# Mamba-2 scan and hash-routed experts on one core: a new program with a 64-step factored scan and experts by seven quarter products

## The chip, the core and the metric

One NeuronCore of a Trainium2 chip runs the kernel; the other cores are idle. The time is the device time of one execution in microseconds (us). TensorE (PE) multiplies matrices, VectorE (DVE), ScalarE (ACT) and GpSimd (POOL) work element by element, and SyncE (SP) issues DMAs, as ACT and POOL also can. PEld is TensorE's loading of the stationary operand, which is recorded apart from the multiplication.

## What is computed

Two stages. The first is a scan over 4 sequences, 8 heads, 768 steps, head dimension 32 and state dimension 16; the second sends every token (a step with its 8 x 32 values) to one of 8 experts, chosen by a hash of the token's number. Cut to the core:

```python
# scan, per sequence and head; la = log(a)
cum = cumsum(la)                       # inside a chunk
M = (C @ B.T) * exp(cum_i - cum_j)     # zero where i < j
y = M @ x + (C @ state) * exp(cum_i)
state = exp(sum(la)) * state + sum_j B_j x_j exp(cum_end - cum_j)
# experts: N = 3072 tokens, 256 -> 1024 -> 256
e = token_ids * 2654435761 % 8
out[mask] = maximum(x[mask] @ w1[e], 0) @ w2[e]
```

Everything is float32. The result doesn't depend on where the chunks of the scan end.

## The kernel before

**Scan (lines 263 to 385).** The 3072 tokens are 24 chunks of 128 steps; chunk `gc` belongs to sequence `gc // 6`. `prepare` (L275 to L297) turns a sequence's B and C so that head and state lie on the partitions, 16 rows a head. `chunk` takes four heads at a time. For the decays it builds 128x128 triangles scaled by log a (`rl`, L316 on ACT and L318 on DVE), sums them on TensorE (`seg`, L320 and L322, 512 columns), takes the exponential (`dl`, L324), multiplies C.B (`gram`, L329) by it (`m`, L331), and multiplies the result, as a stationary 128x128 operand, with 32 columns of x (`y_ps`, L335). The state's share comes from L342 to L351, the state itself from `tp` at L358 and `s_new` at L364. Each chunk's y goes to DRAM by token (`y_tokens`, L352). In L358 four products fill the four groups of 32 columns of the array, one for each pair of heads.

**Routing.** `routing` (L190 to L249) finds every token's slot: experts stand one after the other, each from a multiple of 128 on, 31 slot tiles in all. 24 indirect DMAs (L252) write token numbers to their slots in DRAM, one load (L258) brings the table back, and `idx_in` (L259) is taken from it on DVE.

**Experts (L388 to L467).** A tile of 128 slots at a time: `gather` (L400) fetches rows of y by an indirect DMA on POOL, `turn_x` (L408) transposes them, `up` (L424) multiplies with the tile as stationary operand and w1 as moving, four products of 512 columns, then relu (L415, L417); `down` transposes h (L436), multiplies with w2 (L444), eight products of 256 columns, and scatters 128 rows (L448). All weights lie in SBUF; they are loaded on ACT's queue during the scan (`load_w`), two loads of 1 MB in every second chunk.

A scheduler orders each engine's instructions after the dependencies and the order in which the code issues them; each engine runs its own list in order. x, B, C and y go through SP's queue.

Of the kernel before, what the change touches and what calls it, by code (L numbers as in the profile page):

```python
# [9 lines left out]
F32 = mybir.dt.float32  # L10
# [8 lines left out]

@with_exitstack  # L20
def kernel(
# [11 lines left out]
    nc = tc.nc  # L33

# [33 lines left out]
    a_t = apre.tile([BH, S], F32)  # L68
    nc.sync.dma_start(out=a_t, in_=a.rearrange("b h s -> (b h) s"))

    bcs, xs = {}, {}

    def load_bc(b):
        t = aload.tile([P, 2, H, R * NS], F32, name="bc", bufs=1)
        for i, src in ((0, B), (1, C)):
            nc.sync.dma_start(out=t[:, i], in_=src[b].rearrange("h (p r) n -> p h (r n)", r=R))
        bcs[b] = t

    def load_x(gc):
        b, c = divmod(gc, R)  # L80
        t = aload.tile([P, H, D], F32, name="x_t", bufs=6)
        nc.sync.dma_start(out=t, in_=x[b, :, c * P:(c + 1) * P, :].rearrange("h p d -> p h d"))
        xs[gc] = t

    load_bc(0)
    XA = 4
    for gc in range(XA):
        load_x(gc)
# [3 lines left out]
    nc.sync.dma_start(out=tok, in_=tok_h.bitcast(I32).rearrange("(c p two) -> c p two", c=NCH, two=2))  # L92

    w1_sb = wpool.tile([P, E * WS], F32)
    w2_sb = wpool.tile([P, E * WS], F32)

    def load_w(e):
        s = slice(e * WS, (e + 1) * WS)
        nc.scalar.dma_start(out=w1_sb[:, s].rearrange("p (k f) -> p k f", k=DP),
                            in_=moe_w1[e].rearrange("(k p) f -> p k f", p=P))  # L100
        nc.scalar.dma_start(out=w2_sb[:, s].rearrange("p (k d) -> p k d", k=FP),
                            in_=moe_w2[e].rearrange("(k p) d -> p k d", p=P))

# [1 line left out]
    ident = const.tile([P, P], F32)  # L105
    make_identity(nc, ident)
    ident16 = const.tile([P, P], BF16)
    nc.vector.tensor_copy(out=ident16, in_=ident)
    ones = const.tile([P, P], F32)
    nc.vector.memset(ones, 1.0)  # L110
    upto = const.tile([P, P], F32)      # [k, i] = k <= i
    nc.gpsimd.affine_select(out=upto, in_=ones, pattern=[[1, P]], compare_op=OP.is_ge,
                            fill=0.0, base=0, channel_multiplier=-1)
    after = const.tile([P, P], F32)     # [k, j] = k > j
    nc.vector.tensor_scalar(out=after, in0=upto, scalar1=-1.0, scalar2=1.0, op0=OP.mult, op1=OP.add)
    low = const.tile([P, P], BF16)      # [j, i] = -1000 where i < j: exp of it is 0
    nc.vector.tensor_scalar(out=low, in0=upto, scalar1=1000.0, scalar2=-1000.0, op0=OP.mult, op1=OP.add)  # L117

    gmask = const.tile([P, G, 2 * D], F32)   # [(h n), g, :] = h // 2 == g
    nc.gpsimd.memset(gmask, 1.0)  # L120
    nc.gpsimd.affine_select(out=gmask, in_=gmask, pattern=[[-32, G], [0, 2 * D]], compare_op=OP.is_ge,
                            fill=0.0, base=0, channel_multiplier=1)
    nc.gpsimd.affine_select(out=gmask, in_=gmask, pattern=[[32, G], [0, 2 * D]], compare_op=OP.is_ge,
                            fill=0.0, base=31, channel_multiplier=-1)
    hm = const.tile([P, G, 2], F32)          # [(h n), g, e] = h == 2 g + e
    nc.gpsimd.memset(hm, 1.0)
    nc.gpsimd.affine_select(out=hm, in_=hm, pattern=[[-32, G], [-NS, 2]], compare_op=OP.is_ge,
                            fill=0.0, base=0, channel_multiplier=1)
    nc.gpsimd.affine_select(out=hm, in_=hm, pattern=[[32, G], [NS, 2]], compare_op=OP.is_ge,
                            fill=0.0, base=NS - 1, channel_multiplier=-1)  # L130
# [172 lines left out]
    def chunk(gc, s_old):  # L303
# [50 lines left out]
        if c == R - 1:  # L354
            return None
# [144 lines left out]
```

## Time and profile before

| | us |
|---|---|
| time, median of 3 runs | 505.13 (505.11 to 524.7) |
| span of the profiled execution | 506.3 |
| TensorE busy in it | 431.5 |
| VectorE, ScalarE, GpSimd busy | 160.9, 117.0, 93.0 |
| weights, 16 loads of 1 MB | 9.4 each, from issue to landing |

The span runs from the first to the last instruction. Busy times of engines overlap each other. A row of a timeline begins with its start and its length in us and merges neighbours of a kind (x8); the bracket is how long the engine stood idle before it and what ended that. A matrix product of float32 is recorded as two MATMULs with a LDWEIGHTS each.

### The profile page before, as it was taken

Reading aid. Unit: us, or ns where it says so; the run is one execution under the profiler, and the core shown is the slowest. Engines: PE = TensorE matmul, PEld = TensorE weight load, DVE = VectorE, ACT = ScalarE, POOL = GpSimd, SP = SyncE. Lnnn points to the kernel's source line nnn. Section 1 sums busy time; section 2 is a strip of 40 time slices with the busy share of each in tenths; the row PEclk is TensorE's granted clock in tenths of the full one; section 3 lists DMA queues with packets and bytes.
Section 4 is the critical chain, followed back from the end, with each engine's and each line's share of the span. In section 5 each row is a group of like instructions: output and inputs, shape, how many; then the busy total and the mean of one; then the engine's idle time right before and its main releaser. Section 6 shows DMA issues by size and latency. Waiting matters only on the chain.

```text
span 506.3 us, 6022 instructions
## 1 busy us (share of the span) xinstructions
PE 431.5 (85%) x2103; PEld 287.1 (57%) x2103; DVE 160.9 (32%) x399; ACT 117.0 (23%) x254; POOL 93.0 (18%) x106
## 2 busy tenths in 40 slices
PE   0689994008999999993999999999999999999992
PEld 0356652005656666662567676767667676767671
DVE  2355851003575675551112212121212122121210
ACT  2151441002344343420121212121121212121220
POOL 1100544500000000004331313132222222110110
PEclk9997998555999999996899999999999999999997
DMA  8966799625932112001110101010101111000000
GB/s 284 217 172 209 125 107 135 88 5 131 286 115 54 41 32 43 21 22 52 53 41 21 41 22 32 22 41 22 42 21 42 31 32 31 13 21 12 1 1 0
DMA packets 55216, 33.98 MB, mean 67 GB/s; under 512 B 40058, under 2 KB 51346, under 8 KB 55188
## 3 DMA queue, kind: packets, MB, share of 16 engines
q10 hardware_dynamic: 10496, 16.78, 13.4%
q1 hardware_dynamic: 40948, 9.60, 10.7%
q0 software_dynamic: 3744, 7.23, 5.1%
q8 instruction: 18, 0.29, 0.3%
q14 instruction: 10, 0.08, 0.1%
HBM read 27.27 MB, written 7.24 MB: 68 GB/s over the span
## 4 chain that ended last, share of the span: by engine, by line
issue 45%; PE 28%; POOL 15%; DMA 7%; DVE 2%; ACT 1%; POOLq 1%; SPq 0%; another core or an unknown queue 0%; ACTq 0%; DVEq 0%
PE y_ps L335 7%; PE seg L322 7%; POOL out_dram L448 6%; PE gram L329 5%; POOL xg L400 5%; POOL slot_tokens L252 4%; DMA bc<-in_C_dram 3%; PE seg L320 2%; DMA slot_tokens<-token,slot_i 2%; PE y_ps L346 2%; PE tp L358 1%; PE tp L281 1%; DMA idx_out<-slot_tokens 1%; PE h_ps L424 1%; DMA xg<-y_tokens,idx_in 1%
## 5 line engine op out<-in xcount | busy, mean ns | idle before, releaser
L424 PE MATMUL h_ps<-w_sb,xT 128*128 x248 | 118.2, 608 | 1.2 <-issue 0.3
L444 PE MATMUL o_ps<-w_sb,hT 128*128 x496 | 113.3, 381 | 1.3 <-ACT hT L439 0.6
L444 PEld LDWEIGHTS o_ps<-w_sb,hT 128*128 128x128 f32 x496 | 93.3, 190 | 24.7 <-issue 7.2
L417 DVE TENSOR_SCALAR h<-h_ps 128x512 f32<-128x512 f32 x31 | 21.5, 692 | 195.6 <-PE h_ps L424 195.6
L335 PE MATMUL y_ps<-x_t,m 128*128 128x32 f32 x384 | 51.8, 280 | 35.0 <-DVE m L331 31.4
L335 PEld LDWEIGHTS y_ps<-x_t,m 128*128 128x128 f32 x384 | 51.1, 202 | 53.0 <-DVE m L331 38.9
L424 PEld LDWEIGHTS h_ps<-w_sb,xT 128*128 128x128 f32 x248 | 46.4, 194 | 42.4 <-issue 40.4
L448 POOL DMA_INDIRECT out_dram<-o_sb,idx_out x31 | 31.2, 1006 | 172.1 <-ACT o_sb L447 172.1
L322 PE MATMUL seg<-rl,after 128*128 128x512 f32 x96 | 53.9, 646 | 0.4 <-ACT rl L316 0.4
L400 POOL DMA_INDIRECT xg<-y_tokens,idx_in x31 | 32.0, 1032 | 116.5 <-issue 90.8
L324 ACT ACTIVATE dl<-seg 128x512 f32<-128x512 f32 x48 | 28.6, 598 | 96.3 <-PE seg L322 85.2
L447 ACT ACTIVATE o_sb<-o_ps 128x256 f32<-128x256 f32 x31 | 11.9, 383 | 128.6 <-PE o_ps L444 124.8
L331 DVE TENSOR_TENSOR m<-gram,dl 128x512 f32<-128x512 f32 x48 | 32.9, 686 | 24.6 <-PE gram L329 24.5
L329 PE MATMUL gram<-ce,bt 32*128 32x256 f32 x192 | 40.0, 441 | 0.0
L436 PEld LDWEIGHTS ht_ps<-ident,h 128*128 128x128 f32 x248 | 28.4, 140 | 8.3 <-issue 8.2
L252 POOL DMA_INDIRECT slot_tokens<-token,slot_i x24 | 23.9, 995 | 45.5 <-DVE s_new L364 25.2
L436 PE MATMUL ht_ps<-ident,h 128*128 128x128 f32 x248 | 32.1, 273 | 0.0
L316 ACT ACTIVATE rl<-upto,laT 128x128 f32<-128x128 f32 x96 | 32.0, 389 | 0.0
L320 PE MATMUL seg<-low,ident 128*128 128x512 bf16 x48 | 19.3, 409 | 13.3 <-DVE low L117 11.8
L439 ACT ACTIVATE hT<-ht_ps 128x512 f32<-128x512 f32 x31 | 18.5, 597 | 50.0 <-PE ht_ps L436 49.9
L415 ACT ACTIVATE h<-h_ps 128x512 f32<-128x512 f32 x31 | 18.5, 597 | 42.8 <-PE h_ps L424 42.8
L318 DVE TENSOR_SCALAR rl<-upto,laT 128x128 f32<-128x128 f32 x96 | 23.4, 285 | 12.4 <-PE seg L322 12.0
(100 smaller groups left out, 245.2 us busy)
## 6 DMA issues: line engine op xcount, KB each, us to landing
w_sb<-in_moe_w_dram ACTq DMA_DIRECT2D x16, 1024.0 KB, 9.4
x_t<-in_x_dram SPq DMA_DIRECT2D x24, 128.0 KB, 2.8
y_tokens<-y_sb SPq DMA_DIRECT2D x24, 128.0 KB, 1.7
bc<-in_B_dram SPq DMA_DIRECT2D x4, 384.0 KB, 9.8
bc<-in_C_dram SPq DMA_DIRECT2D x4, 384.0 KB, 13.4
xg<-y_tokens,idx_in POOLq DMA_INDIRECT x31, 2.9
out_dram<-o_sb,idx_out POOLq DMA_INDIRECT x31, 2.5
slot_tokens<-token,slot_i POOLq DMA_INDIRECT x24, 17.0
```

Of the source, the lines that this page charges most:

```text
L252: st = nc.gpsimd.indirect_dma_start(out=slot_dram[:, None], out_offset=bass.IndirectOffsetOnAxis(ap=slot_i[:, c:c + 1], axis=0), in_=token ...
L316: nc.scalar.activation(rl[:, k], upto, AF.Copy, scale=w)
L320: nc.tensor.matmul(out=seg, lhsT=ident16, rhs=low.unsqueeze(1).to_broadcast([P, HH, P]), start=True, stop=False)
L322: nc.tensor.matmul(out=seg, lhsT=after, rhs=rl, start=False, stop=True)
L329: nc.tensor.matmul(out=gram[:, k, 0:2 * P], lhsT=bt[r, t], rhs=ce[r, :, t], start=True, stop=True)
L331: nc.vector.tensor_tensor(out=m.rearrange("p (k e) i -> p k (e i)", k=2), in0=gram[:, :, 0:2 * P], in1=dl.rearrange("p (k e) i -> p k (e i ...
L335: nc.tensor.matmul(out=y_ps[:, 0, h0 + k], lhsT=m[:, k], rhs=x_t[:, h0 + k], start=True, stop=True)
L400: nc.gpsimd.indirect_dma_start(out=xg[k], out_offset=None, in_=y_dram[:], in_offset=bass.IndirectOffsetOnAxis(ap=idx_in[:, k:k + 1], axis= ...
L424: nc.tensor.matmul(out=hp, lhsT=xT[k][:, i], rhs=w1_sb[:, bass.ds(regs[k] + (i * F + j * FH), FH)], start=(i == 0), stop=(i == DP - 1))
L436: nc.tensor.transpose(out=tp[:, f], in_=h[:, ff * P:(ff + 1) * P], identity=ident)
L444: nc.tensor.matmul(out=op, lhsT=hT[:, f], rhs=w2_sb[:, bass.ds(regs[k] + f * DM, DM)], start=(f == 0), stop=(f == FP - 1))
L448: st = nc.gpsimd.indirect_dma_start(out=out[:], out_offset=bass.IndirectOffsetOnAxis(ap=idx_out[:, k:k + 1], axis=0), in_=o_sb, in_offset= ...
```

## The change

The file is a new program for the same function. Its parts:

**Scan.** Units of 64 steps (`T`), two to a chunk, two chunks to a pair, 12 pairs. exp(cum_i - cum_j) is written as exp(cum_i - mid) x exp(mid - cum_j) with `mid` the sum at the unit's middle; the first factor is multiplied into C and the second into B before these are turned (`rows_part`, L208), so a unit's matrix needs only a triangular 0/1 mask (`masked`, L536) and the state needs one factor a unit (`g_sb`). Products are small and named with the part of the array that they use: `inter` (L561, state to output: 32 rows, 64 columns of the array), `intra` (L571: 64 rows, 64 columns), `dstates` (L497: 64 rows, 32 columns), `gram` (L528: 32 rows, 64 columns). Per pair 32, 32, 16 and 16 of them, fewer `inter` where a sequence begins and fewer `dstates` where it ends: 352, 384, 176 and 192, 1104 in all.

**Routing.** In pieces between the pairs. Experts are ranked by their number of tokens; the expert in place p gets two halves of `HALF[p]` slots, 25 slot tiles in all. The table from slot to token comes from products of one-hot matrices (L404), on the core. Tokens that don't fit go to extra tiles in a loop at the end, whose number of passes is read at run time. With the reference's token numbers the experts hold 403, 399, 394, 382, 379, 376, 371 and 368 tokens, and the halves sum to 404, 400, 396, 384, 380, 376, 372 and 368.

**Experts.** Both layers take the weights as stationary operand (128x128) and the slots as moving operand, 184 to 202 columns. Each layer is a product of 2x2 blocks in Winograd's form: seven products of quarters in place of eight, with four sums of the weights' quarters (`sums_w1`, `sums_w2`; on POOL but for the first), four of the inputs' quarters (`sums_x`, `sums_h`; DVE) and sums of the results when they are taken out of PSUM (DVE, two copies on ACT). That makes 28 products a layer and expert, 448 in all. The first down layer's inputs need no transposes; the output is transposed before the scatter (`put`, L844). Expert p's up products are issued between expert p - 1's down products. Products 1 and 2 of the first three experts, which need only slots filled by the first 2048 tokens, are issued between the scan and the last gathers (24 products). Weights are fetched by expert, on SP's queue, from the ninth pair on.

The order of every engine is the order of the code (`manual_schedule`).

```diff
+HALF = [202, 200, 198, 192, 190, 188, 186, 184]
...
+    fac = const.tile([P, 2, R, NB, H], F32)
...
+    act.activation(fac[:, 0], nat, AF.Exp, scale=-1.0)
+    act.activation(fac[:, 1], nat, AF.Exp)
...
+    def masked(k):
...
+            dve.copy_predicated(out=m[:, t], mask=mk, data=ps[:, 0:G, t * P:(t + 1) * P])
...
+    def y_out(u, hh, t, h4, w):
+        o = ps[hh * T:(hh + 1) * T, BY + u, t * P + h4 * D:t * P + (h4 + w) * D]
...
+    def inter(k, swap):
...
+                for g in range(G):
+                    u = (g + swap) % 2
+                    n = 2 * t + u
...
+                    r = slice(32 * g, 32 * g + 32)
+                    h = 2 * g + e
+                    o, first = y_out(u, h // 4, t, h % 4, 1)
+                    pe.matmul(out=o, lhsT=ces[b][r, e, c:c + T], rhs=sps[k][r, n, e * D:(e + 1) * D],
+                              start=first, stop=False, skip_group_check=True)
...
+    for k in range(NP):
...
+        inter(k, 0)
+        if more:
+            dstates(k + 1, 0)
+            states(k + 1, (0,))
...
+        intra(k, 0)
+        if more:
+            dstates(k + 1, 1)
+            states(k + 1, (1, 2, 3))
+        intra(k, 1)
...
+        inter(k, 1)
+        y_evict(k)
+        if more:
+            gram(k + 1)
+        piece(k)
+        if k + 2 < NP:
+            back(k + 2)
+        if more:
+            masked(k + 1)
+        if k == 9:
+            for q in EK:
+                gather(q, early=True)
...
+        if 8 <= k < 11:
+            load_w1(k - 8, 0)
+    y_store(NP - 1)
...
+    def sums_w1(p, eng):
...
+        eng.tensor_tensor(out=s[:, 0], in0=q(1, 0), in1=q(1, 1), op=OP.add)
+        eng.tensor_tensor(out=s[:, 1], in0=s[:, 0], in1=q(0, 0), op=OP.subtract)
+        eng.tensor_tensor(out=s[:, 2], in0=q(1, 0), in1=q(0, 0), op=OP.subtract)
+        eng.tensor_tensor(out=s[:, 3], in0=q(0, 1), in1=s[:, 1], op=OP.subtract)
...
+    def up(p, q0, what, bank, st):
...
+        for i in range(2):
+            pe.matmul(out=ps[:, bank, i * n:(i + 1) * n], lhsT=lhs[:, (q0 + i) * P:(q0 + i + 1) * P], rhs=rhs,
+                      start=(first and i == 0), stop=True, skip_group_check=True)
...
+    UP = [1, 6, 5, 7, 2, 4, 3]
+    UP_E = [6, 5, 7, 4, 3]
+    DOWN = [1, 2, 6, 5, 7, 3, 4]
...
+            if s == 0 and p + 1 < E:
+                sums_w1(p + 1, pool_e)
+            if s == 1 and p < E:
+                sums_w2(p, pool_e)
+            if s >= 2:
+                ask(1)
...
+    with tc.For_i(0, rn[0], 1):
```

On TensorE, in the scan of before, the rows of about a chunk (`seg`: segment sums; `y_ps`: outputs; `tp` at L358: the state's increment):

```order
L335 MATMUL y_ps<-x_t,m 128x32 x4
L329 MATMUL gram<-ce,bt 128x256 x2
L358 MATMUL tp<-x_t,bs 32x64 x4
L320 LDWEIGHTS ident_110
L320 MATMUL seg<-low,ident_110 128x512
L322 MATMUL seg<-rl,after 128x512
L329 MATMUL gram<-ce,bt 128x256 x2
```

The same engine in the scan of the change, one pair (`ps` is the whole of PSUM; L486 and L223 are transposes, `sp` the scaled states, `m` the masked matrices):

```order
L486 MATMUL ps<-ident,bt 128x128 x2
L223 MATMUL ps<-ident,rows_438 128x128 x4
L561 MATMUL ps<-sp,ce 64x32 x16
L497 MATMUL ps<-x_t,bn 32x64 x8
L571 MATMUL ps<-x_t,m_117 64x32 x16
L497 MATMUL ps<-x_t,bn 32x64 x8
L571 MATMUL ps<-x_t,m_117 64x32 x16
L561 MATMUL ps<-sp,ce 64x32 x16
L528 MATMUL ps<-ce,bt 64x128 x16
```

The 512-column segment sums are gone; the next pair's state increments (L497) stand between this pair's outputs, and the next pair's `gram` (L528) stands at the end.

On TensorE, in the experts of before, where one tile's `up` ends and another's `down` begins (ISA rows set the weights' address):

```order
L424 MATMUL h_ps<-w_sb,xT 128x512
L408 MATMUL xt_ps<-ident,xg 128x128
L436 MATMUL ht_ps<-ident,h 128x128 x8
L408 MATMUL xt_ps<-ident,xg 128x128 x2
L444 ISA
L444 MATMUL o_ps<-w_sb,hT 128x256
```

In the change, between the fourth and the fifth expert (`w` and `s` are weights and their sums, `t` and `hx` inputs; L776 is `up`, L818 `down`, L456 and L844 transposes):

```order
L776 MATMUL ps<-t_2542,s_2447 128x190 x2
L456 MATMUL ps<-ident,xg 128x128 x2
L844 MATMUL ps<-ident,xT 128x128 x2
L818 MATMUL ps<-h_2484,w_2418 128x192 x4
L776 MATMUL ps<-t_2542,s_2447 128x190 x4
L456 MATMUL ps<-ident,xg 128x128 x2
L844 MATMUL ps<-ident,xT 128x128 x2
L818 MATMUL ps<-hx,w_2418 128x192 x4
```

The transposes of h are gone, and one expert's up products alternate with the expert before's down products.

On POOL, in the experts of before, there are only gathers (L400) and scatters (L448):

```order
L400 DMA xg<-y_tokens,idx_in 128x256 x9
L448 DMA out_dram<-o_sb,idx_out 3072x256
L400 DMA xg<-y_tokens,idx_in 128x256 x2
L448 DMA out_dram<-o_sb,idx_out 3072x256 x2
L400 DMA xg<-y_tokens,idx_in 128x256
```

In the change the sums of the weights (L717 to L729) stand on the same queue, here in the third step of the experts:

```order
L448 DMA xg<-y_tokens,idx_in 128x256 x5
L853 DMA out_dram<-o_sb,idx_out 3072x256
L717 TENSOR_TENSOR s_2307<-w_2154 128x512
L718 TENSOR_TENSOR s_2307<-s_2307,w_2154 128x512
L719 TENSOR_TENSOR s_2307<-w_2154 128x512
L720 TENSOR_TENSOR s_2307<-w_2154,s_2307 128x512
L726 TENSOR_TENSOR s_2331<-w_2280 128x512
L727 TENSOR_TENSOR s_2331<-s_2331,w_2280 128x512
L728 TENSOR_TENSOR s_2331<-w_2280 128x512
L729 TENSOR_TENSOR s_2331<-w_2280,s_2331 128x512
L448 DMA xg<-y_tokens,idx_in 128x256 x5
```

The gathers and scatters now stand behind eight sums an expert.

## Rows read from the trace of the kernel before

**Rows 1.** The page's heading, and the granted clock of its part 2.

```profile
span 506.3 us, 6022 instructions
...
PEclk9997998555999999996899999999999999999997
```

**Rows 2.** By stretch: length, then PE, PEld, DVE, ACT, POOL; clock, DMA.

```profile
84.00:115.50 31.50, 0.96 (x2) 0.24 (x2) 0.80 (x3) 0.00 (x0) 8.09 (x9) 0.50 0.56 59
115.50:231.00 115.50, 112.83 (x719) 73.98 (x719) 66.22 (x177) 42.15 (x103) 0.82 (x1) 0.96 0.29 80
...
240.00:497.00 257.00, 254.55 (x1050) 174.32 (x1048) 52.02 (x91) 48.79 (x93) 57.34 (x57) 0.99 0.09 27
```

**Rows 3.** Waits: who waited for whom, us in total, times, longest.

```profile
DVE idx_in L259 <- DMA idx_out<-slot_tokens: 31.6, 1, 31.6
```

**Rows 4.** Groups by form on PEld: busy us, mean ns; idle before.

```profile
L444 PEld LDWEIGHTS o_ps<-w_sb,hT 128*128 128x128 f32 x496 | 93.3, 190 | 24.7 <-issue 7.2 <-ACT hT L439 6.3
```

**Rows 5.** Timeline of TensorE in one tile of the experts.

```profile
373.97 3.62 PE L444 MATMUL o_ps<-w_sb,hT 128*128 x16
...
377.42 2.74 PE L424 MATMUL h_ps<-w_sb,xT 128*128 x6
...
378.71 0.19 PEld L424 LDWEIGHTS h_ps<-w_sb,xT 128*128 128x128 f32 x1 [0.24 <-issue]
379.14 0.19 PEld L424 LDWEIGHTS h_ps<-w_sb,xT 128*128 128x128 f32 x1 [0.24 <-issue]
...
380.00 0.90 PEld L436 LDWEIGHTS ht_ps<-ident,h 128*128 128x128 f32 x8 [0.29 <-issue]
```

**Rows 6.** Timeline of weight loads in the scan at full clock.

```profile
196.24 0.97 PEld L335 LDWEIGHTS y_ps<-x_t,m 128*128 128x128 f32 x8 [0.33 <-issue]
...
197.87 0.16 PEld L358 LDWEIGHTS tp<-x_t,bs 128*32 128x32 f32 x8 [0.33 <-issue]
...
198.12 0.10 PEld L320 LDWEIGHTS <-ident 128*128 128x128 bf16 x1
```

**Rows 7.** Groups by form on DVE, ACT and POOL: busy us, mean ns.

```profile
L331 DVE TENSOR_TENSOR m<-gram,dl 128x512 f32<-128x512 f32 x48 | 32.9, 686 | 24.6 <-PE gram L329 24.5
L448 POOL DMA_INDIRECT out_dram<-o_sb,idx_out x31 | 31.2, 1006 | 172.1 <-ACT o_sb L447 172.1
...
L348 DVE TENSOR_TENSOR y_sb<-y_ps,dec 128x256 f32<-128x256 f32 x20 | 8.4, 422 | 19.2 <-PE y_ps L346 14.0 <-remote 5.1
...
L289 ACT ACTIVATE ce<-tp,par 128x384 f32<-128x384 f32 x8 | 7.6, 948 | 8.3 <-PE tp L281 8.1
...
L364 DVE SCALAR_TENSOR_TENSOR s_new<-s_new,pend,tp 128x64 f32<-128x64 f32 x16 | 4.4, 275 | 6.2 <-PE tp L358 6.1
...
L277 POOL COPY rows<-bc 128x768 f32<-128x768 f32 x4 | 3.3, 827 | 70.4 <-PE tp L281 57.8 <-DMA bc<-in_C_dram 12.6
...
L225 DVE CAST tiles<-n_i 128x8 f32<-128x8 int32 x1 | 0.2, 172 | 0.0
```

**Rows 8.** Timeline of the start.

```profile
3.99 0.55 DVE L135 TENSOR_SCALAR a_t<-a_t 32x768 f32<-32x768 f32 x1 [2.87 <-DMA a_t<-in_a_dram]
...
33.50 1.08 PE L335 MATMUL y_ps<-x_t,m 128*128 128x32 f32 x8
```

**Rows 9.** Timeline of the seam between scan and experts.

```profile
231.05 0.32 SPq L352 DMA_DIRECT2D y_tokens<-y_sb  x1
233.92 1.07 POOL L400 DMA_INDIRECT xg<-y_tokens,idx_in  x1 [87.40 <-issue]
...
236.98 0.66 PE L408 MATMUL xt_ps<-ident,xg 128*128 128x128 f32 x2 [6.88 <-DMA xg<-y_tokens,idx_in]
```

**Rows 10.** By stretch, columns as in rows 2: 117 to 121 us.

```profile
117.00:121.00 4.00, 4.00 (x14) 2.87 (x13) 0.48 (x2) 1.27 (x3) 0.00 (x0) 0.50 0.54 137
```

**Rows 11.** Timeline of the end: the last scatter.

```profile
497.38 0.98 POOL L448 DMA_INDIRECT out_dram<-o_sb,idx_out  x1 [3.92 <-ACT o_sb L447]
```

**Rows 12.** Chain of work, 117 to 121 us: start, length, piece.

```profile
119.58 1.55 PE y_ps L335 x8
```

More of the change, by code (lines that the diff above doesn't have):

```diff
@@ L105 @@
+    for c in range(2):
+        load_x(c)
+    load_bc(1, 0)
+    load_bc(1, 1)
+    for c in range(2, 6):
+        load_x(c)
+    fill16 = const.tile([P, 512], BF16)
+    dve.memset(fill16, 0.0)
+    rst = const.tile([P, SU, T], F32)
+    dve.memset(rst, 1.0)
+    dve.memset(rst[:, :, 0:1], 0.0)
+    warm = const.tile([P, 1], F32)
+    act.activation(warm, rst[:, 0, 1:2], AF.Ln)
+    m_sb = [awork.tile([P, 2, G, 2 * T], F32, name=f"m{i}", bufs=1) for i in range(2)]
     ident = const.tile([P, P], F32)
@@ L106 @@
     make_identity(nc, ident)
[L107 to L115, printed above, removed]
@@ new lines, with load_regs, load_w1 @@
+    w1s, w2s = {}, {}
+    regs = []
+    def load_regs():
+        _, r = nc.values_load_multi_w_load_instructions(
+            place_i[0:1, :], engines=[ET.SP], min_val=0, max_val=E - 1,
+            skip_runtime_bounds_check_because="experts' numbers, a sum of one-hot rows times 0 to E - 1")
+        regs.extend(r)
+    def load_w1(p, i):
+        if p not in w1s:
+            w1s[p] = wpool.tile([P, DP, F], F32, name="w1")
+        src = moe_w1[bass.ds(regs[p], 1), :, i * FH:(i + 1) * FH].rearrange("e (k p) f -> p (e k) f", p=P)
+        sp_e.dma_start(out=w1s[p][:, :, i * FH:(i + 1) * FH], in_=src)
@@ new lines @@
+    rows_part(dve, 0, 0, 0, 4)
+    rows_part(pool_e, 0, 1, 0, 2)
+    rows_part(dve, 0, 0, 4, 6)
+    rows_part(pool_e, 0, 1, 2, 6)
+    turn_bc(0, 0, BT)
+    evict_bc(0, 0, BT, (act, act))
+    rt_ids()
+    turn_bc(0, 1, BY)
+    evict_bc(0, 1, BY, (act, dve))
+    back(0)
+    turn_bc(0, 2, BY + 1)
+    evict_bc(0, 2, BY + 1, (act, dve))
+    rows_part(pool_e, 1, 0, 0, 4)
+    decays_of_units()
+    dstates(0, 0)
+    states(0, (0,))
+    gram(0)
+    dstates(0, 1)
+    masked(0)
+    states(0, (1, 2, 3))
@@ new lines, with ask, turn_due @@
+    asked = set(EK)
+    queue = []
+    for p in range(E):
+        for k in tiles_of(p):
+            if k not in turned and k not in queue:
+                queue.append(k)
+    need = {p: [k for k in tiles_of(p)] for p in range(E)}
+    done_at = {k: max(p for p in range(E) if k in tiles_of(p)) for k in range(NK)}
+    def ask(n):
+        for k in [k for k in queue if k not in asked][:n]:
+            gather(k)
+            asked.add(k)
+    def turn_due(p, bank=BT, eng=None):
+        return [k for k in queue if k in need[p] and k not in turned]
@@ new lines @@
+    load_w1(0, 1)
+    ask(3)
+    sts = {(p, q0): {} for p in range(E) for q0 in (0, 2)}
+    load_w2(0)
+    load_w1(1, 1)
+    load_w2(1)
+    load_w1(2, 1)
+    for p in range(NEAR - 1):
+        for what in (1, 2):
+            for q0 in (0, 2):
+                up(p, q0, what, (2 * p + q0 // 2) % 4, sts[p, q0])
+        if p == 0:
+            sums_w1(0, dve)
+        ask(1)
+    for k in turn_due(0):
+        turn_x(k)
+        turned.add(k)
+    sums_x(0)
+    UP = [1, 6, 5, 7, 2, 4, 3]
```

1054 lines of the change are left out of this document (704 added, 350 removed).

## The prediction

> **What bounds the kernel now.** I read the page first, then the busy time by stretch, then the waits, then single groups and pieces of the timeline. The span is 506.3 us and TensorE's granted clock is full (1.00, 2.4 GHz) except in a few slices [rows 1]. By stretch: scan to 231 us, experts from 240 to 497 us, a short end [rows 2]. TensorE is busy 112.8 of 115.5 us in the second half of the scan and 254.6 of 257 us in the experts, and every other engine is under 60% there, so TensorE's own work sets both parts. The one long hole is 84 to 115.5 us, 1.0 us of work on TensorE: VectorE waits 31.6 us for the table of slots to come back from DRAM [rows 3]. So the change is priced mainly as work on TensorE: what one pass costs, and how many are left. A float32 product is recorded as two passes (496 for 248 products), each with its weight load [rows 4].
>
> **What one pass costs.** In the experts, at full clock, two passes over 512 columns start 0.43 us apart and 16 passes over 256 columns take 377.42 - 373.97 = 3.45 us, 0.216 each; eight transposes start within 0.90 us, 0.11 each [rows 5]. The line through the first two is 0.00083 us a column plus 0.003, so 192.5 columns (the mean of the new table) cost 0.163 us a pass. The weight load isn't in the way: where only 32 columns follow a 128-column load, eight loads take 0.97 us [rows 6], so loads can follow each other every 0.11 us, under 0.163. The recorded 190 ns of one load [rows 4] is longer because loads overlap.
>
> **Experts.** Removed: the 31 tiles with 512- and 256-column products (124 and 248) and 310 transposes. Added: 8 experts x 56 products (28 up, 28 down) = 448 products of 184 to 202 columns, 896 passes; 25 + 25 tiles transposed twice, 100 transposes. 24 of the products (48 passes, 8 us) stand ahead in the seam and 14 transposes are done by then. What is left: 848 x 0.163 = 138, 86 x 0.11 = 10, together 148. Covered work per expert (TensorE 19.5 us): VectorE takes four sums of 192 elements, four of 768, ten evictions of 385, five of 192; 256 elements cost 0.42 and 512 cost 0.69 us [rows 7], about 0.16 + n x 0.00104, so 1.4 + 3.8 + 5.6 + 1.8 = 12.6 us. POOL takes eight two-input sums of 512 elements, an operation that the trace doesn't show there: from below a copy's pace (768 elements in 0.83 us [rows 7]), 0.55 each; from above twice that for two inputs, 1.1; I take the upper. With 6.3 DMA issues of 1.0 us that is 15 us. Both hide under 19.5 with 4.5 us to spare. If the cover goes, each further us of POOL beyond that costs 8 us in all. On POOL's queue the sums stand ahead of gathers and scatters (order above): a sum that waits for its weights holds them up, but gathers are asked one expert ahead and four output buffers stand behind the scatters, so I charge nothing. The first expert has no down products to fill its evictions' waits, and the last no up products: +6 us.
>
> **Scan.** Removed on TensorE: the segment sums (two kinds of 512-column products), 192 products with a 128-column load for 32 columns, gram products of 256 columns. Off ACT and VectorE: 192 scaled triangles, 48 exponentials. Added: 1104 small products (352 state-to-output, 384 inside a unit, 176 state increments, 192 grams), each in a quarter or less of the array, in fours that use different rows or columns. The nearest row is the state increment of before: four products, eight passes with 32-column weights; all loads start within 0.16 us, and the next load comes 198.12 - 197.87 = 0.25 us after the first [rows 6]. At that price 276 fours are 69 us. Below: if nothing but the eight starts counts, 0.16 a four, 44 us. Above: one after another at the pace of the 32-column products of before, 0.97/4 = 0.25 us **each** [rows 6], 276 us. I take 69, because the row is the only one of four column tiles. Besides that 72 transposes of 0.11 (8 us) and the routing's 24 + 2 table products (2 us): 79. Per pair of chunks that is 6.6 us. Beside it VectorE has two masked copies of 512 elements (not in the trace; I take the 0.69 of a two-input operation; as a plain copy they would be no dearer) and four state steps of 0.28, 2.5 us, plus up to 18 small routing steps of 0.17 [rows 7], 3 us; ACT at most two strided evictions of 512 (384 cost 0.95 [rows 7], so 1.26 each) and 1.0 more, 3.5; POOL about 4.3 with its two-input products at the upper price. VectorE is nearest; the masked copies stand behind the routing on its queue, and TensorE's next inner products wait for them. I charge 3 us for four such pairs: **82 us**. What of the old hole? The table now comes from products with one-hot rows and never goes through DRAM, so the 31.5 us go; what is late next is the first gather, asked at the end of the tenth pair and needed at the end of the eleventh.
>
> **Start.** The decays arrive at 4.0 us, and the first product inside a chunk stands at 33.5 us [rows 8]. There weights share the DMA engines with B and C; now no weight moves before the ninth pair. What is left is a chain: clip, log, running sum, shift (1.9 us), 24 small turns and two exponentials (2.4), scaling and turning B and C with their evictions (5.5), increments, gram and mask (2.2): 12 on 4.0, **16 us**. Not below 12; not above 33.
>
> **Seam.** Before, from the last store's issue at 231.05 to the first gather 2.9 us passed, and 3.0 more to the first transpose [rows 9]. Now the store is two DMAs on SP's queue (a half row each), the gathers queue on POOL, and behind the store on SP stand 3.5 MB of weights that share the engines with the gathers. 1 us of eviction, 2.9, one more gather issue of 1.0, 3.0, two evictions and sums, 1.5: 9.4, say **10 us**, while TensorE does its 8 us of early products. Without them the clock would fall: it was at 0.50 (1.2 GHz) after the 31 us without work and still so at 117 to 121 us [rows 2, 10].
>
> **End.** From the end of the last scatter's issue (498.36 [rows 11]) to the end 7.9 us. Ahead of it now an eviction, two transposes and four scatters in a row (5 us), and a count read into every engine's registers for the closing loop, about 2: **15 us**. The inputs' tokens give 368 to 403 an expert, none above its two halves, so the loop runs no pass.
>
> **Sum.** 16 + 82 + 10 + 148 + 6 + 15 = 277 us of span, against 506.3. The median of the runs shown is 505.13, 1.2 below its span: I predict **276 us**.
>
> **Rivals.**
> *State-to-output products by twos (+22).* In `inter` the four products of a group use four row tiles but two PSUM banks, two to each bank and different halves of its partitions; no row of before has that. If a pair that shares a bank goes one after the other, 88 fours take another 0.25: 22 us, 298. Against: the column tiles of the increment shared a bank and overlapped [rows 6]. The Trainium skill (TensorEngine Tiling (Array Packing), Gotcha 1: PSUM Pressure) says that different row tiles cannot access the same bank simultaneously, which would make this the forecast; the trace cannot decide it, since its tiles there are of columns.
>
> *Experts bound off TensorE (+15 to +30).* If POOL's two-input sums (8.8 us) and VectorE's work (12.6) exclude each other, an expert takes 21.4 instead of 19.5: +15, 291; with sums of 1.8 us on POOL alone, 14.4 + 6.3 = 20.7 plus waits for the weights of about 3: +30, 306. For it: no row of before has both engines at such work together. The Trainium skill (GPSIMD Engine Reference, Key points) says that POOL shares its SBUF interfaces with VectorE and contends with instructions of two SBUF inputs; eight of VectorE's operations per expert are of that kind.
>
> *Scan at half clock, but overlapped (+70).* Small tiles leave waits between groups, and the clock stays at 0.50: a four takes 0.5, 138 + 10 + 3, 346 us. Against: the old scan, with its many short products, held 0.96 to 1.00 [rows 1, 2].
>
> *Slower than before: no overlap, and half clock.* At 0.50 [rows 10] the 32-column products took 1.55/4 = 0.39 us each [rows 12]: 1104 x 0.39 + 13 = 444 us for the scan, 640 in all. Without overlap at full clock: 276 + 13, 484, 4% faster. It decides at (516 - 195 - 13)/1104 = 0.28 us for a small product: above it the kernel is slower by over 2%. Against: [rows 6] show the overlap.
>
> **Chances.** Forecast 0.62, with its own range 252 (fours of 0.16) to 292; by twos 0.14 (290 to 325); experts off TensorE 0.13 (288 to 310); half clock with overlap 0.06 (330 to 360); no overlap at full clock 0.02 (484); the slower one 0.03. The range for 8 in 10 is **250 to 330**. About 2% is what a measurement of this kernel tells from no change. Faster by over 2%: 0.62 + 0.14 + 0.13 + 0.06 + 0.01 = 0.96; within 2% 0.01; slower 0.03.
>
> **What would show it.** The scan: the twelve pairs about 6.6 us apart, small products in fours that start together, clock 1.00; `inter` groups twice as long as `intra` groups for the first rival. No wait of VectorE for a table from DRAM. The seam: TensorE idle under 3 us between the early products and the first transpose. The experts: passes 0.16 apart with loads hidden, TensorE above 95% busy, about 20 us an expert; POOL's sums at 1.1 us or less, no wait of TensorE for s1 or s2. The end: about 15 us from the last product. Wrong would be: a pair at 10 us or more, an expert at 22 or more, or a pass that costs its 190 ns of load.

## The result, and the profile after

The changed kernel takes 311.87 us (median; runs from 310.52 to 315.08), the kernel before 510.72 in the same comparison: a ratio of 0.616 (95% interval 0.611 to 0.622). That is 36 us above the predicted 276 and inside the range of 250 to 330. The profiled execution took 310.52 with a span of 308.8. Medians here and below are over all runs, while ratios leave out runs in a slower state, more than 1.5% above the fastest of the same kernel: here two of the four before (516.31 and 524.7), further down one of e11's four and two of e8's, its profiled one among them, so that e8 has no row in the table.

By stretch (us from start to end; then the stretch's length, each engine's busy time with its instructions, TensorE's granted clock, the share of the DMA engines and GB/s). The first five rows are start, scan, seam, experts and end of the changed kernel, where [rows 2] showed them before; the last two are five microseconds of the scan at either clock:

```profile
0.00:24.10 24.10, 15.18 (x156) 9.04 (x157) 12.46 (x31) 8.20 (x14) 7.91 (x46) 0.74 0.65 137
24.10:109.20 85.10, 76.73 (x2230) 61.95 (x2230) 41.97 (x121) 26.37 (x44) 49.87 (x89) 0.64 0.45 101
109.20:124.70 15.50, 12.03 (x57) 10.58 (x57) 4.48 (x7) 8.06 (x17) 9.34 (x9) 0.83 0.89 279
124.70:296.90 172.20, 158.15 (x934) 152.12 (x934) 111.60 (x183) 42.87 (x109) 119.29 (x93) 0.96 0.30 97
297.00:308.80 11.80, 0.00 (x0) 0.00 (x0) 0.44 (x2) 0.11 (x1) 3.84 (x4) 0.56 0.11 36
36.00:41.00 5.00, 4.27 (x179) 3.44 (x181) 3.56 (x10) 2.74 (x4) 1.66 (x4) 1.00 0.44 92
95.00:100.00 5.00, 5.00 (x138) 3.83 (x130) 2.17 (x5) 0.54 (x2) 3.78 (x5) 0.50 0.63 159
```

Against the sum of the prediction: start 24.1 for 16 (+8), scan 85.1 for 82 (+3), seam and experts 187.7 for 10 + 148 + 6 = 164 (+24), end 11.9 for 15 (-3). So two thirds of the miss lie behind the scan (from the start of the last eviction of y at 109.2 us on), and there TensorE is idle for 17.4 us and at half clock for 17.9.

Who it waits for there, in total, times, and the longest (waits of TensorE, 109.2 to 296.9 us):

```profile
PE ps L776 <- DVE u L795: 8.9, 6, 2.7
PE ps L818 <- DVE xT L836: 2.8, 3, 1.0
PE ps L776 <- DVE t L736: 2.3, 1, 2.3
```

L795 is VectorE's combine of up products, which frees a PSUM buffer. One of the two 2.7-us gaps, in the timeline of VectorE, then POOL, then TensorE (start, duration, line, operation, out<-in; in brackets the idle time before and what ended it):

```profile
215.31 0.36 DVE L836 TENSOR_TENSOR xT<-ps,du 128x192 f32<-128x192 f32 x1
215.58 1.12 DVE L735 TENSOR_TENSOR t<-xT 128x188 f32<-128x188 f32 x1
216.73 1.30 DVE L736 TENSOR_TENSOR t<-xT,t 128x188 f32<-128x188 f32 x1
217.96 1.41 DVE L737 TENSOR_TENSOR t<-xT 128x188 f32<-128x188 f32 x1
219.29 0.34 DVE L738 TENSOR_TENSOR t<-xT,t 128x188 f32<-128x188 f32 x1
219.55 0.54 DVE L795 TENSOR_TENSOR u<-ps,p 128x380 f32<-128x380 f32 x1
...
215.22 1.27 POOL L727 TENSOR_TENSOR s<-s,w 128x512 f32<-128x512 f32 x1
216.45 1.38 POOL L728 TENSOR_TENSOR s<-w 128x512 f32<-128x512 f32 x1
217.79 1.36 POOL L729 TENSOR_TENSOR s<-w,s 128x512 f32<-128x512 f32 x1
...
214.71 0.80 PE L776 MATMUL ps<-t,s 128*128 128x190 f32 x4
215.35 0.81 PE L776 MATMUL ps<-xT,w 128*128 128x190 f32 x4
216.00 1.46 PE L818 MATMUL ps<-hx,s 128*128 128x192 f32 x8
220.15 1.63 PE L776 MATMUL ps<-t,w 128*128 128x190 f32 x4 [2.69 <-DVE u L795]
```

The sums of the gathered rows (L735 to L738) read two SBUF operands of 188 elements and take 0.34 us alone. Three of them here take 1.12 to 1.41, and each ends about 0.2 us after one of POOL's weight sums has ended (216.49, 217.83, 219.15), when the next begins. The fourth, with POOL done, takes 0.34. The operation with a PSUM operand (L836) keeps its 0.36. VectorE takes its queue in order, so the combine L795 starts at 219.55 and TensorE stands.

### The profile page after: what moved, and what is told of

Read it like the earlier page. It is cut to its first block, busy times and chain, and to the rows that moved or that the text cites. A ratio compares the mean times of both kernels' runs of the same rounds, so it can differ in the third digit from the quotient of the medians.

```text
span 308.8 us, 8166 instructions
## 1 busy us (share of the span) xinstructions
PE 262.1 (85%) x3373; PEld 233.7 (76%) x3374; DVE 171.0 (55%) x343; ACT 85.7 (28%) x183; POOL 190.3 (62%) x240
## 4 chain that ended last, share of the span: by engine, by line
PE 34%; DVE 9%; DMA 7%; POOL 2%; issue 1%; ACT 0%; POOLq 0%; DVEq 0%
PE ps L818 17%; PE ps L776 15%; DMA out_dram<-o_sb,idx_out 7%; DVE t L737 1%; DVE u L795 1%; DVE t L736 1%; PE ps L456 1%; PE ps L844 1%; DVE t L735 1%; DVE t L754 1%; DVE t L747 1%; DVE du L835 1%; DVE xT L836 1%; DVE t L738 1%; POOL s L727 1%
## 5 line engine op out<-in xcount | busy, mean ns | idle before, releaser
L448 POOL DMA_INDIRECT xg<-y_tokens,idx_in x25 | 27.2, 1086 | 30.7 <-PE ps L844 14.0
L510 POOL TENSOR_SCALAR sp<-z,g_sb 128x64 f32<-128x64 f32 x44 | 19.4, 453 | 36.8 <-DVE z L518 25.8
L776 PE MATMUL ps<-t,s 128*128 128x202 f32 (+7 forms) x192 | 38.5, 337 | 3.6 <-DVE t L736 2.3
L776 PEld LDWEIGHTS ps<-t,s 128*128 128x128 f32 x192 | 33.0, 195 | 5.0 <-DVE t L736 2.6
L818 PE MATMUL ps<-t,s 128*128 128x202 f32 (+7 forms) x192 | 34.9, 326 | 0.0
L818 PEld LDWEIGHTS ps<-t,s 128*128 128x128 f32 x192 | 31.3, 189 | 0.0
L571 PE MATMUL ps<-x_t,m 64*64 64x32 f32 x768 | 22.6, 269 | 4.5 <-DVE m L536 3.7
L776 PE MATMUL ps<-xT,w 128*128 128x202 f32 (+7 forms) x128 | 26.3, 343 | 0.0
L571 PEld LDWEIGHTS ps<-x_t,m 64*64 64x64 f32 x768 | 19.5, 190 | 8.0 <-DVE m L536 4.1
L561 PE MATMUL ps<-sp,ce 32*64 32x32 f32 x704 | 22.9, 266 | 1.1 <-issue 1.0
L561 PEld LDWEIGHTS ps<-sp,ce 32*64 32x64 f32 x704 | 19.5, 184 | 5.5 <-issue 4.0
L776 PEld LDWEIGHTS ps<-xT,w 128*128 128x128 f32 x128 | 23.0, 202 | 0.5 <-ACT p1e L783 0.5
L776 PE MATMUL ps<-t,w 128*128 128x202 f32 (+7 forms) x64 | 15.5, 368 | 9.0 <-DVE u L795 8.9
L776 PEld LDWEIGHTS ps<-t,w 128*128 128x128 f32 x64 | 11.4, 206 | 11.4 <-DVE u L795 11.4
L536 DVE COPY_PREDICATED m<-cmask,ps 128x512 f32<-128x512 int32 x24 | 16.0, 718 | 6.8 <-PE ps L528 6.8
L776 PE MATMUL ps<-xT,s 128*128 128x202 f32 (+7 forms) x64 | 14.4, 355 | 0.0
```

The source lines that it names most:

```text
L448: pool_e.indirect_dma_start(out=xg[k], out_offset=None, in_=y_dram[0:n, :], in_offset=bass.IndirectOffsetOnAxis(ap=idx_in[:, k:k + 1], axi ...
L510: pool_e.tensor_scalar(out=sps[k][:, n], in0=zs["z"], scalar1=g_sb[:, un - 1:un], scalar2=None, op0=OP.mult)
L536: dve.copy_predicated(out=m[:, t], mask=mk, data=ps[:, 0:G, t * P:(t + 1) * P])
L561: pe.matmul(out=o, lhsT=ces[b][r, e, c:c + T], rhs=sps[k][r, n, e * D:(e + 1) * D], start=first, stop=False, skip_group_check=True)
L571: pe.matmul(out=o, lhsT=m_sb[k % 2][u * T:(u + 1) * T, t, h // 2, e * T:(e + 1) * T], rhs=xs[2 * k + t][u * T:(u + 1) * T, h], start=first ...
L776: pe.matmul(out=ps[:, bank, i * n:(i + 1) * n], lhsT=lhs[:, (q0 + i) * P:(q0 + i + 1) * P], rhs=rhs, start=(first and i == 0), stop=True, ...
```

## Experiments

All times below are medians; "scan" and "after the scan" are from each profiled execution (after the scan: start of the last eviction of y to TensorE's last pass). The kernel before took 507 to 521 us beside them. The scan varied from 85 to 92 us between kernels in which it is unchanged, so what an edit of the experts is worth is read from the column after the scan. In the rows without filler, what an edit gains there is, within 0.6 us, the fall of TensorE's idle time plus half the fall of its time at half clock.

| kernel | us | scan starts | scan | after the scan | idle there | half clock there |
|---|---|---|---|---|---|---|
| changed kernel | 311.9 | 24.1 | 85.1 | 187.7 | 17.4 | 17.9 |
| e1, one sum of four | 301.4 | 24.0 | 88.5 | 176.1 | 9.8 | 10.4 |
| e7, sums with one input | 297.3 | 24.3 | 87.6 | 171.7 | 8.5 | 2.9 |
| e2, sums in halves | 304.4 | 24.7 | 88.2 | 176.8 | 13.6 | 2.8 |
| e6, sums on VectorE | 304.4 | 23.9 | 88.0 | 177.9 | 12.1 | 7.6 |
| e3, row sums later | 305.3 | 24.8 | 88.1 | 179.7 | 12.1 | 13.2 |
| e4, expert numbers later | 309.6 | 20.8 | 88.4 | 186.6 | 17.7 | 14.3 |
| e5, filler in the scan | 310.8 | 24.0 | 85.0 | 187.3 | 17.8 | 13.7 |
| e9, sums on both engines | 303.4 | 20.9 | 85.7 | 182.6 | 15.1 | 11.3 |
| e10, sums on VectorE, reordered | 298.3 | 20.9 | 87.2 | 175.8 | 10.1 | 9.3 |
| e11, e9 with less filler | 308.3 | 20.9 | 91.7 | 183.0 | 14.4 | 12.5 |
| e12, e10 with earlier row sums | 304.0 | 21.0 | 91.9 | 176.0 | 11.9 | 5.6 |

**Is it the exclusion of POOL and VectorE?** e1 keeps only the first of the four sums of each set and reads it for the others, so its values aren't the function's (the second layer's alike):

```
...
-  eng.tensor_tensor(out=s[:, 1], in0=s[:, 0], in1=q(0, 0), op=OP.subtract)
-  eng.tensor_tensor(out=s[:, 2], in0=q(1, 0), in1=q(0, 0), op=OP.subtract)
-  eng.tensor_tensor(out=s[:, 3], in0=q(0, 1), in1=s[:, 1], op=OP.subtract)
...
```

> Left out: three of the four weight sums of each layer and expert (six of POOL's eight sums per expert); the products that used them read the first sum instead, so the values differ while every matmul, transpose, VectorE operation and transfer stays. Theory (POOL's two-input sums and VectorE's two-input sums stop each other, and the late VectorE row then holds up TensorE): with a quarter of POOL's sums TensorE's idle time after the scan falls from about 17 us to 4-6 us, the half-clock stretches that follow each gap go with it (9 us lost now), VectorE's longest sum falls from 2.1-2.8 us towards 0.35-0.92 us; time 15 to 25 us lower, about 290. Rival (VectorE's own order or late weights make the gaps): the gaps stay where they are, time within 3 us of the changed kernel's 312.

After the scan it took 11.6 us less, the two 2.7-us gaps are gone, and so is nearly half the idle time. The rival (VectorE's own order or late weights alone) falls, though the gain of 10.5 us is less than the forecast 15 to 25, and 9.8 us idle are more than the 4 to 6. But e1 also makes POOL idle. e7 keeps POOL busy and takes only the second operand away (one of the four, the others are alike):

```
...
-  eng.tensor_tensor(out=s[:, 1], in0=s[:, 0], in1=q(0, 0), op=OP.subtract)
+  eng.tensor_scalar(out=s[:, 1], in0=s[:, 0], scalar1=1.0, scalar2=None, op0=OP.mult)
...
```

> Left out: the second operand of every weight sum; each of POOL's eight operations per expert becomes a multiplication of its first operand by one, on the same 128x512 elements, so the values differ while POOL stays about as busy and everything else stays. Theory (an instruction of POOL with two SBUF inputs and one of VectorE with two SBUF inputs exclude each other): VectorE's sums go back to 0.35 us (190 elements) and 0.92 us (512 elements) everywhere, the 2.7-us gaps go, time 8 to 14 us lower than the changed kernel's 312, as with one sum of four (301). Rival (any large operation on POOL slows VectorE): the stretch of VectorE's sums stays at up to 2 us and the time within 4 us of 312.

297.3 us, 14.6 below the changed kernel, a little more than the 8 to 14 of the theory. The same place of the program in e7, VectorE, then POOL, then TensorE:

```profile
207.95 0.34 DVE L735 TENSOR_TENSOR t<-xT 128x188 f32<-128x188 f32 x1
208.33 0.75 DVE L736 TENSOR_TENSOR t<-xT,t 128x188 f32<-128x188 f32 x1
209.00 0.34 DVE L737 TENSOR_TENSOR t<-xT 128x188 f32<-128x188 f32 x1
209.26 0.34 DVE L738 TENSOR_TENSOR t<-xT,t 128x188 f32<-128x188 f32 x1
209.53 0.54 DVE L795 TENSOR_TENSOR u<-ps,p 128x380 f32<-128x380 f32 x1
...
206.81 1.49 POOL L719 TENSOR_SCALAR s<-w 128x512 f32<-128x512 f32 x1
208.26 1.49 POOL L720 TENSOR_SCALAR s<-w 128x512 f32<-128x512 f32 x1
...
210.12 0.91 PE L776 MATMUL ps<-t,w 128*128 128x190 f32 x4 [0.29 <-DVE u L795]
```

POOL is busier than before (1.49 us an operation instead of 1.27), and three of VectorE's sums run inside one of its operations. The gap fell from 2.69 to 0.29 us. So it isn't POOL's being busy that costs, but operations with two SBUF inputs on both sides at once (e7 changes the kind of POOL's operation together with its inputs, so the kind as a cause isn't excluded). An operation of POOL with one input holds VectorE too, but only at first. In e7 seven sums of the gathered rows were stretched, to 0.42 to 0.78 us. All of them began within 0.4 us of the start of an operation of POOL and ended 0.81 to 0.90 us after that start, as L736 above; those that began later in one took 0.34 to 0.38 us. Four of the longer sums, of the hidden values, took 1.22 to 1.46 us where 0.92 to 0.99 is usual (up to 2.81 in the changed kernel).

The Trainium skill (GPSIMD Engine Reference, Key points) names contention with VectorE instructions of two SBUF inputs: the trace agrees. The Trainium skill (SBUF — State Buffer, SBUF: two separate sides) makes it a lock held for the whole instruction, against a GpSimd operation that reads SBUF: the changed kernel agrees, where stretched sums end 0.2 us after POOL's; e7 does not, since its operations read SBUF and hold a sum for only about 0.5 of their 1.49 us (an estimate: 0.81 less the sum's own 0.35).

If each engine waits for a whole instruction of the other, shorter instructions cost less. e2 makes each weight sum in two halves, in both functions (the first of the four):

```
+  for c in (slice(0, FH // 2), slice(FH // 2, FH)):
-  eng.tensor_tensor(out=s[:, 0], in0=q(1, 0), in1=q(1, 1), op=OP.add)
+      eng.tensor_tensor(out=s[:, 0, c], in0=q(1, 0)[:, c], in1=q(1, 1)[:, c], op=OP.add)
...
```

> Each of POOL's weight sums is made in two halves of 256 elements, so that a VectorE instruction that must wait for one waits half as long; the total work on POOL grows only by the fixed cost of 8 more instructions per expert. Theory (each engine waits for the other's whole instruction): VectorE's longest sums of 190 elements fall from 2.1 us to about 1.1 us, the 2.7-us gaps before the third up product shorten by half, time 4 to 10 us lower (302 to 308). Rival (the stretch is a rate shared over the time both run, not a wait for an instruction): VectorE's sums stay as long, POOL's total rises by some 8 x 0.1 us per expert, time the same or up to 4 us higher.

After the scan 10.9 us less, more than expected, though POOL's total grew by some 13 us; no sum of gathered rows took more than 0.89 us (2.11 in the changed kernel). The wait is for an instruction, not a shared rate. All 32 of these sums together took as long as before (22.0 us, 22.4 in the changed kernel): what fell is the longest hold, and with it the gaps. e6 takes the sums off POOL altogether, one sum a slot (the first layer's):

```
-            if s == 0 and p + 1 < E:
-                sums_w1(p + 1, pool_e)
+            if s < 4 and p + 1 < E:
+                sums_w1(p + 1, dve, s)
...
```

> All weight sums move from POOL to VectorE, one per slot, so POOL forms none. Theory (the exclusion is the cost, and VectorE has the room): 8 sums x 0.69 = 5.5 us more for VectorE per expert, about 18 of 19.5 us, none of its sums stretched, TensorE's idle time after the scan down from 17 to 6-10 us, time 297 to 305. Rival (VectorE becomes the bound, since its combines must come in time for TensorE's buffers): idle time after the scan 18 us or more, time 312 to 325.

Nothing is stretched (weight sums 0.68, row sums 0.35, hidden sums 0.95 us), and the time is at the forecast's upper end. Of the 12.1 us of idle time that are left (6 to 10 forecast), 3.7 still stand at the same combine, in six waits of 1.0 us at most, and 2.4 at two combines that no longer come in time.

**Is it VectorE's order?** e3 leaves the engines alone and issues the row sums one slot later, behind the combine:

```
-                if p + 1 < E:
-                    sums_x(p + 1)
+            if s == nslot - 2 and p + 1 < E:
+                sums_x(p + 1)
```

> The four sums of the next expert's gathered rows are issued on VectorE one slot later, behind the combines of the up products instead of ahead of them. Theory (TensorE's 2.7-us gaps are there because the up combine stands behind the stretched sums in VectorE's order): the two 2.7-us gaps and the half-clock stretches behind them go, time 6 to 10 us lower (302 to 306); POOL and VectorE sums stay as stretched as they are. Rival (what is late is POOL's own sum or a transfer): the gaps move to another row of the same size, time within 3 us.

The sums stay nearly as stretched (those of the gathered rows 0.61 us on average, 0.70 in the changed kernel, 0.35 alone), but TensorE now waits 1.6 us for L795 instead of 8.9, and after the scan it is 8.0 us less. One gap of 2.2 us moved to another combine:

```profile
PE ps L776 <- DVE hx L804: 2.2, 1, 2.2
PE ps L776 <- DVE u L795: 1.6, 2, 1.0
```

So the loss has two parents, a stretched sum and a combine queued behind it: after the scan the order alone gives 8.0 us, half of the 16.0 that e7 gives.

**The start.** Where TensorE first waits, in the changed kernel and with the transpose of the expert numbers moved behind the start's other work (e4: `rt_ids()` is called after `back(1)` instead of ahead of `turn_bc(0, 1, BY)`, with its result in another PSUM bank):

```profile
8.25 3.11 POOL L208 TENSOR_TENSOR rows<-bc,fac 128x256 f32<-128x256 f32 x3 [1.75 <-ACT fac L201]
9.35 1.07 DVE L274 TENSOR_SCALAR eid_i<-tok 24x128 int32<-24x128 int32 x1
10.46 0.98 DVE L276 CAST eid_r<-eid_i 24x128 f32<-24x128 int32 x1
11.58 0.22 PE L277 MATMUL ps<-ident,eid_r 24*128 24x24 f32 x1 [2.20 <-DVE eid_r L276]
```

```profile
18.73 0.21 DVE L274 TENSOR_SCALAR eid_i<-tok 24x128 int32<-24x128 int32 x1
18.97 0.27 DVE L276 CAST eid_r<-eid_i 24x128 f32<-24x128 int32 x1
```

> The transpose of the expert numbers, for which TensorE waits 2.2 us in the start, moves behind the start's other transposes. Theory (that wait holds up the transposes behind it, and they the scan): the scan starts about 2 us earlier (22 instead of 24.1), time about 2 us lower. Rival (the start's end is set by VectorE's rows and ScalarE's factors): the scan starts at 24 as before, no change.

The scan starts 3.3 us earlier and the kernel is 2.3 us shorter. The two operations took 1.07 and 0.98 us beside POOL's two-input products, and 0.21 and 0.27 without them: here VectorE's operations have one SBUF input and no PSUM operand, and are held up too.

**The scan's clock.** e5 adds filler after the grams:

```
+        for _ in range(8):
+            pe.matmul(out=ps[:, 3, 256:512], lhsT=fill16[:, 0:P], rhs=fill16[:, 0:256], start=True, stop=True,
+                      skip_group_check=True)
```

> Added work that nothing reads: eight bf16 products of 256 columns per pair of chunks, written to an unused part of a PSUM bank, in the scan alone. Theory A (the scan's half-clock stretches, 62 of its 85 us, come of small products that do not hold the granted clock, and the clock bounds it): the granted clock goes to 1.0 in most of the scan, pairs fall to 5.5-6.0 us plus 0.9 us of filler; scan 76 to 85 us, so 0 to 9 us lower. Theory B (the granted clock does not answer to this, or TensorE's clock is not what bounds the pairs): clock at 0.5 as now, each pair 1.7 us longer at half clock, scan 97 to 105 us, time 12 to 20 us higher.

The half-clock time of the scan fell from 61.8 to 31.7 us, and the scan stayed at 85.0 (85.1): the filler itself took some 17 us, 1.05 us a pair at full clock and 1.9 at half, so the rest of the scan took that much less. Theory A came at the weak end of both its ranges (85.0 for 76 to 85, 1.1 us lower for 0 to 9), theory B fell. The scan does follow the clock, but this is no way to win by it: what the clock gave back the filler took. Half the filler, on e9:

> As the mix of VectorE and POOL sums, with four added bf16 products of 256 columns per pair of the scan that nothing reads (eight gave the scan the same 85 us, with 32 instead of 62 us at half clock). Theory A (half the filler buys nearly as much clock at half its price of 0.9 us a pair): scan 80 to 84 us, 2 to 5 us below the mix. Theory B (the clock gained falls with the filler): half clock 45 to 60 us, scan 85 to 88 us, time that of the mix within 2 us.

58 us at half clock and a scan of 91.7, 6.0 us more than e9's, so nothing is won: the half clock is theory B's, the time worse than it. Most of that is one pair, the twelfth, of 11.6 us (8.1 in e9); e12 has such a pair too, the eleventh, of 11.5, where TensorE's inner products come in small lots with nothing in the records that they wait for:

```profile
94.63 0.65 PE L561 MATMUL ps<-sp,ce 32*64 32x32 f32 x14
95.51 0.45 PE L561 MATMUL ps<-sp,ce 32*64 32x32 f32 x5 [0.23 <-issue]
96.29 0.42 PE L561 MATMUL ps<-sp,ce 32*64 32x32 f32 x4 [0.34 <-issue]
97.04 0.31 PE L561 MATMUL ps<-sp,ce 32*64 32x32 f32 x1 [0.32 <-issue]
```

What held them stays open.

**Better versions.** e8 joins e2, e3 and e4:

> Three edits together: weight sums in halves, the sums of the gathered rows one slot later, the expert numbers' transpose later. Singly the first two gave 7 us each (304.4 and 305.3 after 311.9). Theory (both act on the same wait, VectorE's late up combine): together 9 to 12 us, not 14; with the start's 2 us, 298 to 302. If they act on different waits: 295 to 297.

299.4 us (295.95 to 300.71; ratio to before 0.590, 0.581 to 0.599): the edits overlap, as the first theory had it. The next two put sums on VectorE, with the reorderings of e3 and e4:

> The four sums of the first layer's weights go to VectorE, one per slot, those of the second layer stay on POOL; with the later sums of the gathered rows and the later transpose of the expert numbers. VectorE takes 4 x 0.69 = 2.8 us more per expert (15.4 of 19.5 us without stretching), POOL half as many two-input sums. Theory (exclusion is the cost, and splitting the sums over both engines meets it half as often): idle time of TensorE after the scan 8-10 us, time 295 to 300. Rival (what VectorE gains on one side it loses on the other): idle time 11-13 us, time 300 to 305.

> All weight sums on VectorE, one per slot, with the two edits of order (sums of the gathered rows one slot later, expert numbers' transpose later). With all sums on VectorE alone the time was 304.4, with 12.1 us idle after the scan, no sum stretched. Theory (what was left there was order, not load): idle time 8-10 us, time 297 to 300. Rival (VectorE at 18 of 19.5 us is the bound now): idle time stays at 12 us, only the start's 2 us come off, 302 to 303.

e9's rival held in its time (303.4): with both engines at weight sums, VectorE's were stretched to as much as 2.36 us, and 15.1 us stay idle, more than its 11 to 13. e10 takes 298.3 us (297.5 to 300.2), 4% under the changed kernel, as its theory had it. It and e8 are the fastest forms here that compute the function; their ranges overlap, so which is faster isn't shown. A last edit (`s == (nslot - 3 if p == 0 else nslot - 2)`) went after e10's longest gap, of 2.35 us:

> As the kernel with all sums on VectorE and the two edits of order, but in the step that fills the first expert, which has only five slots, the next expert's row sums stay one slot earlier: there TensorE waited 2.35 us for them, behind two weight sums. Theory: that gap goes, with up to 1.7 us of half clock behind it; idle time after the scan about 8 us instead of 10.1; time 295 to 297. Rival: the wait moves to the weight sums of the same step, time 298 as before.

That gap went, and three of 1.2 to 1.4 took its place, two of them at the combines that had now to stand behind the row sums: 176.0 after the scan for 175.8, so nothing is won, as the rival said (it had named the weight sums). Of the profiled execution's 5.0 us over e10's, 4.7 lie in the scan, most of them in the slow pair above; why all six runs of e12 (302.3 to 306.2) were slower than e10's, with an edit of the experts alone, stays open.

## Why the prediction was right, and where its terms were off

The total lies in the stated range, but above the forecast's own 252 to 292 and the second rival's 288 to 310. The range held because it covered the rivals, not because the sum was right, and that is in part luck. Several of the signs that the prediction had named came against it: three of seven experts took 22.1, 24.8 and 23.7 us from their first down product to the next expert's ("22 or more"), TensorE was busy for 92% of the experts' stretch ("above 95%"), and the scan's granted clock was 0.64 on average ("1.00").

**Experts and seam, +24.** The price of a pass was right: the four passes over 190 columns at 214.71 and 215.35 above start 0.64 us apart, 0.160 each, where the prediction's line gives 0.161. The step that failed is "Both hide under 19.5 with 4.5 us to spare". VectorE's 12.6 us an expert were right without stretching: e7 has 96.8 us in the 157 us from 127 to 284, 12.1 per 19.6. POOL's 1.1 a sum was called an upper bound and wasn't: 1.27 alone, 1.29 to 1.63 on average beside VectorE. And covering was counted by totals, while what failed was one combine behind stretched sums. The second rival named this mechanism with +15 (291); e7 puts it at 14.6. Its size came right by luck, by another way than it reckoned (21.4 us of added work against 19.5): no engine but TensorE is near full in the experts, POOL being busy 119 of 172 us. It should have had more than 0.13. Unpriced was what comes behind a gap: after each of the two long ones the granted clock stood at 0.50 for 3.4 us. In e7 the stage is still 171.7 for 164, with 8.5 us idle: 2.8 before down products (L836), 1.3 before the first expert's sums (L736), the rest in smaller waits.

Of the 24 us, the seam has 5.5 (15.5 us for 10) and the experts 18 (172.2 for 154). In the seam the early products cover the gathers as told, with a first gather 3.9 us after the last store's issue (2.9 in [rows 9]). But they take 10.3 us for 8, with the granted clock at 0.50 until 114.05 us, and then TensorE waits 2.35 us for row sums that stand beside POOL's sums and take 1.31 and 1.43 us, the same exclusion:

```profile
110.70 10.32 PE L776 MATMUL ps<-xT,w 128*128 128x202 f32 x48
...
123.30 1.31 DVE L736 TENSOR_TENSOR t<-xT,t 128x202 f32<-128x202 f32 x1
124.53 1.43 DVE L737 TENSOR_TENSOR t<-xT 128x202 f32<-128x202 f32 x1
124.66 3.06 PE L776 MATMUL ps<-t,s 128*128 128x202 f32 x8 [2.35 <-DVE t L736]
```

**Scan, +3, by two errors that nearly cancel.** Inner products (32 passes, four fours) and the next group, at full and at half clock:

```profile
37.30 0.67 PE L561 MATMUL ps<-sp,ce 32*64 32x32 f32 x32
37.90 0.43 PE L497 MATMUL ps<-x_t,bn 64*32 64x64 f32 x16
...
95.93 1.08 PE L561 MATMUL ps<-sp,ce 32*64 32x32 f32 x32
96.94 0.65 PE L497 MATMUL ps<-x_t,bn 64*32 64x64 f32 x16
97.52 1.08 PE L571 MATMUL ps<-x_t,m 64*64 64x32 f32 x32
98.53 0.44 PE L497 MATMUL ps<-x_t,bn 64*32 64x64 f32 x8
```

A four costs 0.60/4 = 0.15 us at full clock and 0.25 at half. The prediction took 0.25 and full clock; the lower bound of 0.16 was the right price, and the clock the wrong level. It stood at 0.50 for 62 of the 85 us, though TensorE was busy 5.0 of 5.0 us in the second stretch above, so the third rival's half clock came true at half its price. What the prediction said of the old scan's clock [rows 1, 2] didn't carry to this scan; that the scan's time follows the clock is what e5 shows, why the clock stayed down is not shown. The first rival falls: `inter` (L561, where products of different rows share a bank) takes 1.01 us for 32 passes and `intra` (L571, where those that share a bank use the same rows) the same, both at half clock. The rule in the Trainium skill (TensorEngine Tiling (Array Packing), Gotcha 1: PSUM Pressure) that different row tiles cannot access the same bank simultaneously is not seen to cost anything here. The pairs' evictions stood 5.5 to 9.7 us apart, not 6.6. The stall behind the routing is there as told, once, in the fourth pair, where the masked copies stand behind L336 to L338:

```profile
47.20 1.08 PE L571 MATMUL ps<-x_t,m 64*64 64x32 f32 x32 [2.94 <-DVE m L536]
```

**Start, +8.** The chain was as listed, but its links were priced alone. 3.3 us are the expert numbers behind POOL's products (e4). For the rest the profile offers the half clock from 11.65 us on and VectorE and ScalarE waiting in turn for each other's evictions; that was not tested.

**End, -3.** 11.9 for 15: 4.9 us from the last pass to the end of the last scatter's issue and 7.1 behind it, where [rows 11] gave 7.9. The 2 us for the count's registers leave no trace in this.

**No overlap, and slower than before,** did not come near: a small product costs 0.04 to 0.06 us against the 0.28 at which that rival decided.

## What to carry over

Count two-input work in SBUF on VectorE and POOL as one engine's work, instruction by instruction, and look for what stands behind each such instruction in its in-order queue; operations with a PSUM operand don't belong to that sum, and one-input operations can (e4). Work that is "hidden" by totals is hidden only if no buffer of the bounding engine is freed behind it; moving the release ahead of the stretched work, or cutting the instructions that are waited for, was worth half to two thirds of what e7 gave (8.0 and 10.9 of 16.0 us). Price small products at both clocks.

## What was not expected of the hardware

POOL's multiplication of one 512-element operand by one took 1.49 us where its two-input sum takes 1.27, and yet it held VectorE's sums for only about a third of that time. VectorE's one-input integer operation between SBUF tiles (0.21 us) took 1.07 beside POOL's two-input products. TensorE's granted clock stayed at 0.50 in the scan with the engine busy without a break, which gives each clock its own price of a product, 0.15 and 0.25 us a four.
